# Attention on one core: x transposed by its own DMA, weights loaded in pieces, accumulator banks opened by zero passes, five more tiles on VectorE

## The chip, the cores and the metric

The kernel runs on one core of one Trainium2 chip. The metric is device time in microseconds (us), the median of several executions. "Span" is the time from the first to the last instruction of the one execution that was profiled; it is about 1.8 us shorter than the time that the same execution is given in the list of times. In the lines of the profile PE is TensorE, ACT is ScalarE, DVE is VectorE and SP is SyncE; a q behind the name stands for the engine's sequencer.

## The reference

Sixteen heads of 28 columns each, over 2048 rows of x:

```
x: (1, 2048, 448) bf16, wqkv: (448, 1344) bf16, wo: (448, 448) bf16
qkv = x @ wqkv                     # q, k, v: 16 heads x 2048 x 28
scores = q k^T * 28**-0.5
p = softmax(scores)
out = (p @ v) @ wo
```

## The kernel before

The program is a list of operations with dependencies. A small scheduler in the kernel's own source puts them in order for each engine at build time, so a change in one place can reorder all engines.

The work is cut into 16 units (four heads, 512 query rows), each unit into 16 x 4 tiles of 128 keys x 512 queries. There are 1024 tiles in all. TensorE makes the scores of a tile. ScalarE takes the exponential of two or three tiles with one instruction; VectorE computes it for single tiles by a polynomial of seven operations. TensorE then multiplies the result by V into the unit's accumulator bank (below: the weighted sum).

Before the first exponential can run, x and the weights have to come in, x has to be transposed, and Q and K of the first unit have to be computed. Before the change the transposing is TensorE's work, and the results are copied out of the accumulator memory by VectorE and ScalarE:

```python
XG = 4
xv = xf.rearrange("(n p) d -> p n d", p=128)
...
    dma_x.append(P.add("sp", (lambda e: e.dma_start(x_nat[:, n0:n1, :], xv[:, n0:n1, :])), ...))      # 4 loads of 512 rows
for t, en, prio in ((1, "act", -20), (0, "act", -19), (2, "sp", -7.5)):                               # K, Q, V weights, whole
    dma_w[t] = P.add(en, (lambda e, t=t: e.dma_start(w_raw[0:IT, :, t * D:(t + 1) * D], wview[:, :, t * D:(t + 1) * D])), ...)
...
def tr_job(n0, it, prio, eng):
    def f(e, b):
        for j in range(4):
            ins = e.transpose(bank_bf(b)[0:IT, j * 128:(j + 1) * 128],
                              x_nat[:, n0 + j, it * IT:(it + 1) * IT], id_b[:, :])
        return ins
    xt_ev[(it, n0 // 4)] = job(f"xT{it}_{n0}", prio, [(f, [id_b_op, dma_x[n0 // 4]], "f", 1.1)], ..., evac_eng=eng, ...)
```

TensorE starts slow in these traces: in the kernel before, the first matmuls of zeros start every 0.43 us in groups of four, and every 0.21 us once the clock's own record sets in, at full speed, at 5.25 us. Such a group is here called a zero pass: four matmuls that add nothing to a bank. They are there to get the clock up and to keep it up. Nine passes stand at the start. Others are put into TensorE's idle gaps, and only while some accumulator bank is open: a bank is opened by the operation that has `opens` set and shut by the last sum of its unit.

```python
def zeros(e, b, start, n):
    for i in range(n):
        for h in range(4):
            ins = e.matmul(ps[32 * h:32 * h + 32, b * 512:(b + 1) * 512], ZW[:, :], ZM[:, :], start=start and i == 0, stop=False, ...)
    return ins
warm = P.add("pe", lambda e: zeros(e, 7, True, NWARM), deps=[ms_zw, ms_zm], ..., name="DUMW")      # NWARM = 9
...
def fill(self, zeros, bank_of):
    for k, op in enumerate(pe):
        if k and cur is not None:          # a gap is filled only while a bank is open
            ...
        if op.opens:
            cur = op
        if op.shuts:
            cur = None
...
op = P.add("pe", f_pv, ..., name=f"PV{u}_{kt}", acq=(("M" if u else "A0", 1) if kt == 0 else None), ...)
op.opens = kt == 0                         # the unit's first weighted sum opens its bank
op.shuts = kt == NK - 1
```

At its end the kernel checks its own result (a flag), and every engine branches on it: past the fallback program if the flag is good. A hint, some operations ahead of the branch, announces it:

```python
HINT = {"pe": 40, "act": 8, "dve": 12, "pool": 0, "sp": 4}
...
def body(e, eng):
    n = len(F.order[e])
    F.emit_engine(e, eng, fs, 0, max(n - HINT[e], 0))
    hint = eng.mark_branch_hint_location() if HINT[e] is not None else None
    F.emit_engine(e, eng, fs, max(n - HINT[e], 0), n)
    eng.wait_ge(fs["dve"], F.flag_op.count)
    ok = eng.value_load(F.flag_ap)
    eng.br_ne(ok, 0, f"done_{e}", f"redo_{e}").branch_hint(hint)
    with nc.body(f"redo_{e}", ...):
        ...                                # the fallback program
    nc.switch_bb(f"done_{e}")
```

## Time and profile before

| | us |
|---|---|
| median (424.91 to 425.98, 3 runs) | 425.12 |
| span of the profiled run | 423.67 |
| head: start to the first exponential | 10.87 |
| stream: start of the first exponential to the end of the last | 401.97 |
| tail: from there to the end of the span | 10.83 |

The division into head, stream and tail is read from ScalarE's records. It carries the whole argument, because ScalarE is the limit for the whole stream. First the page of the profiled run: the span, the chain of waits by engine, and the group of ScalarE's exponentials (line, engine, operation, output<-input, shapes, count | busy us, mean ns | idle us before them and what ended it).

```profile
span 423.7 us, 10347 instructions
...
ACT 94%; PE 3%; DVE 1%; issue 0%
...
L842 ACT ACTIVATE PT<-ps 128x1536 bf16<-128x1536 f32 (+1 forms) x309 | 402.0, 1932 | 1.1 <-PE ps L826 1.1
```

ScalarE makes 94% of the chain and is idle 1.1 us in all before its 309 exponentials. The page's mean of one (1932 ns) counts overlap with the next; the starts of two neighbours lie 1.330 us apart for three tiles and 0.903 us for two (medians of the records). The groups kept apart by form show how many there are of each kind:

```profile
L842 ACT ACTIVATE PT<-ps 128x1536 bf16<-128x1536 f32 x278 | 373.7, 2016 | 0.0
...
L842 ACT ACTIVATE PT<-ps 128x1024 bf16<-128x1024 f32 x31 | 28.5, 1179 | 1.1 <-PE ps L826 1.1
```

The two-tile form is the dearer one for each tile: 0.452 us against 0.443 us. Now the start of the chain that ended last (start us, us, what):

```profile
1.21 4.96 PE ps L450 x52
6.17 0.07 issue
6.25 0.42 PE ps L500 x4
6.66 0.02 issue
6.68 0.44 DVE xT L488
...
7.65 1.94 PE ps L517 x32
9.59 0.02 issue
9.61 0.70 DVE KT L488
...
10.45 0.45 PE ps L826 x4
10.89 393.09 ACT PT L842 x303
```

L450 are the zero passes, L500 the transposes of x, L517 the first projections, L826 the first scores. The landings in the trace's DMA records put the first 512 rows of x at 6.11 us. The end is read from what SyncE, which ends the program, waited for (engine, line, what it waited for: us in total, times, longest us):

```profile
SPq L1577 <- PEq L1577: 3.4, 1, 3.4
```

This is the barrier at the end. The view names TensorE's sequencer. The instruction records say otherwise: VectorE came last. Its branch ended at 419.15 us and its next instruction, a drain, started at 423.39 us, 4.24 us later. ScalarE took 0.41 us for the same step.

### The profile page before, as it was taken

The page shows a single profiled execution, that of the slowest core. Times are in us where ns is not written, and L with a number is a line of the kernel's source. Part 1 is how long each engine was busy: PE and PEld are TensorE (multiplying, and loading weights), DVE is VectorE, ACT ScalarE, POOL GpSimd, SP SyncE. Part 2 cuts the span into 40 slices and gives each one's busy share as a digit, 9 for nine tenths or more (in the row PEclk, how much of TensorE's full clock was granted, in tenths as well). Part 3 has the DMA queues.
Part 4 walks back from the last instruction along what each step waited for, and adds up shares of the span by engine and source line. Part 5 has one row for each costly group of instructions (what it writes and reads, how often), then busy time and mean ns, then how long its engine had stood idle before and what let it go on. Part 6 is the DMA issues. An engine that isn't in the chain of part 4 may idle for free.

```text
span 423.7 us, 10347 instructions
## 1 busy us (share of the span) xinstructions
PE 389.0 (92%) x4566; PEld 123.7 (29%) x4566; DVE 380.9 (90%) x650; ACT 406.6 (96%) x316; POOL 3.4 (1%) x9
## 2 busy tenths in 40 slices
PE   8999899999999899899999989998999999999992
PEld 3442232332223233233323222222322223222220
DVE  3436999999999999999999999999999999999953
ACT  2999999999999999999999999999999999999991
POOL 3000000000000000000000000000000000000000
PEclk9999999999999999999999999999999999999997
DMA  8200010101001000010101001010100102010101
GB/s 255 68 0 2 10 26 3 27 2 29 2 4 27 2 27 2 8 22 4 27 3 29 2 3 27 3 28 24 48 3 2 37 15 48 2 29 12 35 27 48
DMA packets 13849, 10.28 MB, mean 24 GB/s; under 512 B 5932, under 2 KB 11820, under 8 KB 13800
## 3 DMA queue, kind: packets, MB, share of 16 engines
q1 hardware_dynamic: 12872, 8.78, 7.7%
q10 hardware_dynamic: 928, 0.80, 0.7%
q8 instruction: 36, 0.59, 0.6%
q14 instruction: 13, 0.11, 0.1%
HBM read 7.50 MB, written 2.08 MB: 23 GB/s over the span
## 4 chain that ended last, share of the span: by engine, by line
ACT 94%; PE 3%; DVE 1%; issue 0%
ACT PT L842 94%; PE ps L450 1%; PE ps L678 1%; PE ps L517 0%; PE ps L773 0%; PE ps L500 0%; PE ps L826 0%; DVE ONX L720 0%; DVE KT L488 0%; DVE OUTS L702 0%; DVE OX L717 0%; DVE xT L488 0%; DVE OTN L722 0%; DVE ZM L444 0%; DVE RS L719 0%
## 5 line engine op out<-in xcount | busy, mean ns | idle before, releaser
L842 ACT ACTIVATE PT<-ps 128x1536 bf16<-128x1536 f32 (+1 forms) x309 | 402.0, 1932 | 1.1 <-PE ps L826 1.1
L826 PE MATMUL ps<-QT,KT 28*128 28x512 bf16 x1024 | 154.6, 384 | 20.5 <-ACT PT L842 15.6
L450 PE MATMUL ps<-ZM,ZW 128*32 128x512 bf16 x1620 | 122.9, 389 | 1.2 <-DVE ZM L444 1.2
L869 DVE TENSOR_SCALAR DT<-ps 128x512 int32<-128x512 f32 x128 | 87.8, 686 | 5.9 <-PE ps L826 4.8
L773 PE MATMUL ps<-PT,V 128*32 128x512 bf16 x896 | 82.2, 384 | 3.0 <-DVE PD L890 1.5
L826 PEld LDWEIGHTS ps<-QT,KT 28*128 28x128 bf16 x1024 | 38.8, 91 | 155.9 <-ACT PT L842 118.9
L890 DVE SCALAR_TENSOR_TENSOR PD<-DT,DL 128x1024 int16<-128x1024 int32 x64 | 77.8, 1216 | 0.0
L450 PEld LDWEIGHTS ps<-ZM,ZW 128*32 128x32 bf16 x1620 | 33.0, 96 | 57.0 <-issue 44.0
L773 PE MATMUL ps<-PD,V 128*32 128x512 bf16 x128 | 46.9, 385 | 0.2
L887 DVE TENSOR_TENSOR DL<-DQ,DL 128x1024 f16<-128x1024 f16 x64 | 43.8, 684 | 0.6
L879 DVE TENSOR_SCALAR DW<-DT 128x1024 f16<-128x1024 uint16 x64 | 43.9, 686 | 0.1
L881 DVE TENSOR_TENSOR DQ<-DW 128x1024 f16<-128x1024 f16 x64 | 43.4, 678 | 0.1
L517 PE MATMUL ps<-xT,w_raw 112*32 112x512 bf16 x512 | 36.8, 383 | 1.0 <-DVE DT L869 1.0
L773 PEld LDWEIGHTS ps<-PT,V 128*32 128x32 bf16 x896 | 20.6, 94 | 38.9 <-issue 17.7
L883 DVE TENSOR_SCALAR DL<-DW 128x1024 f16<-128x1024 f16 x64 | 26.6, 415 | 0.0
L885 DVE TENSOR_SCALAR DQ<-DQ 128x1024 f16<-128x1024 f16 x64 | 26.5, 414 | 0.0
L678 PE MATMUL ps<-wop,OTN 128*128 128x448 bf16 x64 | 15.8, 356 | 2.3 <-DVE OTN L722 1.9
L488 DVE CAST KT<-ps 128x512 bf16<-128x512 f32 x16 | 11.0, 687 | 7.4 <-PE ps L517 7.3
L534 PE MATMUL ps<-w_raw,xT 112*128 112x112 bf16 x256 | 17.1, 214 | 0.0
L488 DVE CAST V<-ps 128x448 bf16<-128x448 f32 x16 | 9.9, 616 | 6.9 <-PE ps L534 6.9
L517 PEld LDWEIGHTS ps<-xT,w_raw 112*32 112x32 bf16 x512 | 10.8, 95 | 16.5 <-issue 7.0
L534 PEld LDWEIGHTS ps<-w_raw,xT 112*128 112x128 bf16 x256 | 13.0, 98 | 6.5 <-issue 4.1
(39 smaller groups left out, 89.3 us busy)
## 6 DMA issues: line engine op xcount, KB each, us to landing
RB<-scr_r SPq DMA_DIRECT2D x60, 64.0 KB, 2.1
x_nat<-in_x_dram SPq DMA_DIRECT2D x4, 448.0 KB, 7.7
out_dram<-OUTS SPq DMA_DIRECT2D x16, 112.0 KB, 1.7
w_raw<-in_wqkv_dram ACTq DMA_DIRECT2D x2, 392.0 KB, 5.6
w_raw<-in_wqkv_dram SPq DMA_DIRECT2D x1, 392.0 KB, 8.8
wop<-in_wo_dram SPq DMA_DIRECT2D x16, 24.5 KB
scr_l<-OTS SPq DMA_DIRECT2D x15, 8.0 KB
LT<-scr_l SPq DMA_DIRECT2D x15, 8.0 KB, 1.7
```

Source lines behind the costliest of these rows:

```text
L450: ins = e.matmul(ps[32 * h:32 * h + 32, b * 512:(b + 1) * 512], ZW[:, :], ZM[:, :], start=start and i == 0, stop=False, tile_position=(0, ...
L517: ins = e.matmul(ps[32 * h:32 * h + 32, b * 512:(b + 1) * 512], w_raw[0:IT, it, col:col + 32], xT[0:IT, it, c * 512:(c + 1) * 512], start= ...
L534: ins = e.matmul(ps[:, b * 512 + j * GD:b * 512 + (j + 1) * GD], xT[0:IT, it, n * 128:(n + 1) * 128], w_raw[0:IT, it, 2 * D + g * GD:2 * D ...
L773: ins = e.matmul(ps[32 * h:32 * h + 32, b * 512:(b + 1) * 512], V[:, kt, hh * 32:(hh + 1) * 32], p_ap, start=(kt == 0 and u > 0), stop=(kt ...
L826: ins = e.matmul(bank(b), KT[32 * h:32 * h + rows, g, kt * 128:(kt + 1) * 128], QT[32 * h:32 * h + rows, g, c * QCH:(c + 1) * QCH], start= ...
L842: ex = P.add("act", (lambda e, p0=p0, w=w, b0=b0: e.activation(PT[:, p0 * 512:(p0 + w) * 512], bank(b0, w), AF.Exp, scale=ESCALE)), deps=[ ...
L869: o1 = P.add("dve", (lambda e, T=T, s=s: e.tensor_scalar(T, bank(s.banks[0]), ZLO, -ZLO, ALU.max, ALU.add)), deps=[s, d_last[di]], dur=610 ...
L879: o2 = P.add("dve", (lambda e, F16=F16, W=W: e.tensor_scalar(W, F16, 1.0 / 65536.0, -0.5, ALU.mult, ALU.add)), deps=[d[2] for d in d_open] ...
L881: o3 = P.add("dve", (lambda e, W=W, Q=Q: e.tensor_tensor(Q, W, W, ALU.mult)), deps=[o2], dur=70 + 540 * k2, prio=pr, name=f"D3_{gi}")
L883: o4 = P.add("dve", (lambda e, W=W, L=L: e.tensor_scalar(L, W, EB, EA, ALU.mult, ALU.add)), deps=[o2], dur=70 + 270 * k2, prio=pr, name=f" ...
L887: o6 = P.add("dve", (lambda e, Q=Q, L=L: e.tensor_tensor(L, Q, L, ALU.mult)), deps=[o4, o5], dur=70 + 540 * k2, prio=pr, name=f"D6_{gi}")
L890: o7 = P.add("dve", (lambda e, T=T, L=L, out=out: e.scalar_tensor_tensor(out, T, 1.0 / 512.0, L, ALU.mult, ALU.add)), deps=[o6] + [slot_la ...
```

## The change

The intent: spare TensorE the transposes and VectorE and ScalarE the copies, bring the weights of the first unit first, let VectorE take five tiles more (133) and keep the first unit's exponentials wider, keep TensorE's clock up by more zero passes, and announce VectorE's branch earlier. The diff, cut to its core:

```diff
-    FILL_TARGET = 0.45
+    FILL_TARGET = 0.48
+    FILL_EARLY = 0.7
+    FILL_UNTIL = 15000.0
-    NWARM = 9
+    NWARM = 16
-        x_nat = sb("x_nat", [128, NST, D], BF16)
-            dma_x.append(P.add("sp", (lambda e: e.dma_start(x_nat[:, n0:n1, :], xv[:, n0:n1, :])), ...
-        for t, en, prio in ((1, "act", -20), (0, "act", -19), (2, "sp", -7.5)):
-            dma_w[t] = P.add(en, (lambda e, t=t: e.dma_start(w_raw[0:IT, :, t * D:(t + 1) * D], ...
+        for c in range(NCH):
+            P.add("sp", (lambda e, rows=rows: e.dma_start_transpose(xT[:, 0:NIT - 1, rows], xf[rows, 0:128 * (NIT - 1)])), ...
+            dma_x.append(P.add("sp", (lambda e, rows=rows: e.dma_start_transpose(xT[:, NIT - 1, rows], xf[rows, XL:D])), ...
+        ...                                   # Q and K weights of the first four heads: ScalarE's queue, first
+        load_w("v", 2 * D, 3 * D, "act", -28)
+        load_w("k", D + W0, 2 * D, "sp", -15)
+        load_w("q", W0, D, "sp", -14)
-        def tr_job(n0, it, prio, eng): ...    # transposes, copies and the identity are gone
-        dve_load[0] += 22.0
+        dve_load[0] += 8.0
-            return ((2, 2), (3, 2), (3, 3))[phase(cur[0])][k % 2]
+            return ((3, 2), (3, 2), (3, 3))[phase(cur[0])][k % 2]
-                                   p_ap, start=(kt == 0 and u > 0), stop=(kt == NK - 1), ...
+                                   p_ap, start=False, stop=(kt == NK - 1), ...
+            if kt == 0 and u:
+                op0 = P.add("pe", (lambda e: zeros(e, acc(u), True, 1)), deps=early_ev + mid_ev, after=[last_pv[0]], ...
+                            name=f"OPEN{u}", acq=("M", 1), acq_slack=ASLACK)
+                op0.opens = True
-HINT = {"pe": 40, "act": 8, "dve": 12, "pool": 0, "sp": 4}
+HINT = {"pe": 40, "act": 8, "dve": 30, "pool": 0, "sp": 4}
```

Left out are the pools of banks in the first unit, the padded layout of the weights (448 rows as three blocks of 128 and one of 64, with zeros from GpSimd), and a correction of the scheduler's times.

More of the change, by code (lines that the diff above doesn't have):

```diff
@@ L204, in schedule @@
                     lat = self.SYNC_LAT
-                ready_t[u] = max(ready_t[u], done_t + lat + (ops[u].slack if isdep else 0.0))
+                ready_t[u] = max(ready_t[u], (done_t if isdep else op.t1) + lat + (ops[u].slack if isdep else 0.0))
                 npred[u] -= 1
@@ L245, in fill @@
                     lo = min(activity(mid - f * self.FILL_SPAN, mid + (1 - f) * self.FILL_SPAN) for f in (0.15, 0.5, 0.85))
-                    if lo + n * one / self.FILL_SPAN >= self.FILL_TARGET:
+                    if lo + n * one / self.FILL_SPAN >= (self.FILL_EARLY if mid < self.FILL_UNTIL else self.FILL_TARGET):
                         break
@@ L330, in _fast @@
     G = H // 4
-    IT = 112
-    NIT = D // IT
+    NIT = 4
+    XL = D - 128
+    W0 = 120
     NST = S // 128
@@ L347, in _fast @@
     ESCALE = 1.0 / (65536.0 * LOG2E)
-    assert DH * H == D and G * 4 == H and DH + 1 <= 32 and NIT * IT == D and GD <= IT
+    assert DH * H == D and G * 4 == H and DH + 1 <= 32 and 128 * (NIT - 1) + 64 == D and GD + 4 <= W0
     xf = x.rearrange("b s d -> (b s) d")
@@ L384, in _fast @@
         OUTS = sb("OUTS", [128, NOB, D], BF16)
-        iota_i = sb("iota_i", [128, 128], I32)
-        id_f = sb("id_f", [128, 128], FP32)
-        id_b = sb("id_b", [128, 128], BF16)
         CK1 = sb("CK1", [128, NU * 16], FP32)
@@ L404, in i32v @@
             return ap.bitcast(I32)
-        XG = 4
-        xv = xf.rearrange("(n p) d -> p n d", p=128)
-        wview = wqkv.rearrange("(it p) c -> p it c", p=IT)
         dma_x = []
-        def load_x(i, prio):
-            n0, n1 = i * NST // XG, (i + 1) * NST // XG
-            dma_x.append(P.add("sp", (lambda e: e.dma_start(x_nat[:, n0:n1, :], xv[:, n0:n1, :])),
-                               dur=400, prio=prio, name=f"dma_x{i}", dma_group=_DmaGroup(f"x{i}"), nbytes=(n1 - n0) * 128 * D * 2))
@@ L416, in _fast @@
-        for i in range(XG):
-            load_x(i, -10 + i)
-        dma_w = {}
-        for t, en, prio in ((1, "act", -20), (0, "act", -19), (2, "sp", -7.5)):
-            dma_w[t] = P.add(en, (lambda e, t=t: e.dma_start(w_raw[0:IT, :, t * D:(t + 1) * D], wview[:, :, t * D:(t + 1) * D])),
-                             dur=400, prio=prio, name=f"dma_w{t}", dma_group=_DmaGroup(f"w{t}"), nbytes=D * D * 2)
-        io_op = P.add("pool", lambda e: e.iota(iota_i[:, :], [[1, 128]], base=0, channel_multiplier=-1),
-                      dur=300, prio=-12, name="iota")
@@ L426, in _fast @@
-        id_f_op = P.add("dve", lambda e: e.tensor_scalar(id_f[:, :], iota_i[:, :], 0.0, None, ALU.is_equal),
-                        deps=[io_op], dur=250, prio=-10, name="id_f")
-        id_b_op = P.add("dve", lambda e: e.tensor_copy(id_b[:, :], id_f[:, :]), deps=[id_f_op], dur=150, prio=-10, name="id_b")
+        for c in range(NCH):
+            rows = slice(c * QCH, (c + 1) * QCH)
+            grp = _DmaGroup(f"x{c}")
+            P.add("sp", (lambda e, rows=rows: e.dma_start_transpose(xT[:, 0:NIT - 1, rows], xf[rows, 0:128 * (NIT - 1)])),
+                  dur=500, prio=-20 + c, name=f"dma_xa{c}", dma_group=grp, nbytes=QCH * 384 * 2)
+            dma_x.append(P.add("sp", (lambda e, rows=rows: e.dma_start_transpose(xT[:, NIT - 1, rows], xf[rows, XL:D])),
+                               after=[P.ops[-1]], dur=500, prio=-20 + c, name=f"dma_xb{c}", dma_group=grp, nbytes=QCH * 128 * 2))
@@ new lines, in _fast, with load_w @@
+        dma_w = {}
+        def load_w(key, c0, c1, en, prio):
+            grp = _DmaGroup(f"w{key}")
+            wv = wqkv[0:128 * (NIT - 1), c0:c1].rearrange("(it p) c -> p it c", p=128)
+            P.add(en, (lambda e: e.dma_start(w_raw[:, 0:NIT - 1, c0:c1], wv)), dur=400, prio=prio, name=f"dma_wa{key}", dma_group=grp, nbytes=(c1 - c0) * 768)
+            dma_w[key] = P.add(en, (lambda e: e.dma_start(w_raw[64:128, NIT - 1, c0:c1], wqkv[128 * (NIT - 1):D, c0:c1])),
+                               after=[P.ops[-1]], dur=400, prio=prio, name=f"dma_wb{key}", dma_group=grp, nbytes=(c1 - c0) * 128)
@@ new lines, in _fast @@
+        grp0 = _DmaGroup("w0")
+        for t in range(2):
+            wv0 = wqkv[0:128 * (NIT - 1), t * D:t * D + W0].rearrange("(it p) c -> p it c", p=128)
+            w0a = P.add("act", (lambda e, t=t, wv0=wv0: e.dma_start(w_raw[:, 0:NIT - 1, t * D:t * D + W0], wv0)), after=P.ops[-1:] if t else [], dur=400, prio=-30,
+                        name=f"dma_w0a{t}", dma_group=grp0, nbytes=W0 * 768)
+        wv1 = wqkv[128 * (NIT - 1):D, 0:2 * D].rearrange("p (t c) -> p t c", t=2)[:, :, 0:W0]
+        wd1 = w_raw[64:128, NIT - 1, 0:2 * D].rearrange("p (t c) -> p t c", t=2)[:, :, 0:W0]
@@ L429, in _fast @@
+        dma_w["q0"] = dma_w["k0"] = P.add("act", (lambda e: e.dma_start(wd1, wv1)), after=[w0a], dur=400, prio=-30, name="dma_w0b", dma_group=grp0, nbytes=2 * W0 * 128)
+        load_w("v", 2 * D, 3 * D, "act", -28)
+        load_w("k", D + W0, 2 * D, "sp", -15)
+        load_w("q", W0, D, "sp", -14)
+        ms_w = P.add("pool", lambda e: e.memset(i32v(w_raw[0:64, NIT - 1, :]), 0), dur=800, prio=-12, name="ms_w")
         V4 = V.rearrange("p n (hh r) -> p (n hh) r", r=32)
@@ L440, in _fast @@
                 dma_wo.append(P.add("sp", (lambda e, g=g, r0=r0, p0=p0: e.dma_start(wop[p0:p0 + DH, g, :], wo[r0:r0 + DH, :])),
-                                    deps=[ms_wop], after=dma_wo[-1:] + dma_x[-1:], dur=300, prio=-5, name=f"dma_wo{g}{h}", dma_group=grp_wo))
+                                    deps=[ms_wop], after=dma_wo[-1:] + [dma_x[-1], dma_w["q"]], dur=300, prio=-5, name=f"dma_wo{g}{h}", dma_group=grp_wo))
         ms_zw = P.add("dve", lambda e: e.memset(i32v(ZW[:, :]), 0), dur=60, prio=-30, name="ms_zw")
@@ L452, in zeros @@
             return ins
-        warm = P.add("pe", lambda e: zeros(e, 7, True, NWARM), deps=[ms_zw, ms_zm], kind="c", units=2.0 * NWARM, prio=-30, name="DUMW")
+        warm = P.add("pe", lambda e: zeros(e, 7, True, NWARM), deps=[ms_zw, ms_zm], kind="c", units=1.0 * NWARM, prio=-30, name="DUMW")
         warm.opens = True
-        P.pool("E", [4, 5, 6])
-        P.pool("J", [5, 6])
+        warm.cells = 1.0 * NWARM
+        P.pool("E", [5, 6])
         P.pool("M", [6, 7])
@@ L463, in _fast @@
         mid_ev = []
-        cur_pool = ["J"]
+        cur_pool = ["E"]
         gated = []
@@ L492, in job @@
             return ev
-        xt_ev = {}
-        def tr_job(n0, it, prio, eng):
-            def f(e, b):
-                ins = None
-                for j in range(4):
-                    ins = e.transpose(bank_bf(b)[0:IT, j * 128:(j + 1) * 128],
-                                      x_nat[:, n0 + j, it * IT:(it + 1) * IT], id_b[:, :])
-                return ins
-            xt_ev[(it, n0 // 4)] = job(f"xT{it}_{n0}", prio, [(f, [id_b_op, dma_x[n0 // 4]], "f", 1.1)],
-                                       ((lambda: xT[0:IT, it, n0 * 128:(n0 + 4) * 128]), (lambda b: bank_bf(b)[0:IT, 0:512])),
-                                       True, evac_eng=eng, evac_dur=600 if eng == "act" else 420)
         kq_ev = {}
@@ L510, in proj_qk @@
             dst = KT if t == 1 else QT
+            wk = "qk"[t] + ("0" if g == 0 else "")
             mms = []
@@ L516, in f @@
                         col = t * D + g * GD + h * DH
-                        ins = e.matmul(ps[32 * h:32 * h + 32, b * 512:(b + 1) * 512], w_raw[0:IT, it, col:col + 32],
-                                       xT[0:IT, it, c * 512:(c + 1) * 512], start=(it == 0), stop=(it == NIT - 1), tile_position=(0, 32 * h))
+                        ins = e.matmul(ps[32 * h:32 * h + 32, b * 512:(b + 1) * 512], w_raw[:, it, col:col + 32],
+                                       xT[:, it, c * 512:(c + 1) * 512], start=(it == 0), stop=(it == NIT - 1), tile_position=(0, 32 * h))
                     return ins
-                mms.append((f, [xt_ev[(it, c)]] + ([dma_w[t]] if it == 0 else []), "c", 1.0))
+                mms.append((f, ([dma_x[c], ms_w, dma_w[wk]] if it == 0 else []), "c", 1.0))
             kq_ev[(t, g, c)] = job(f"p{t}_{g}_{c}", prio, mms,
@@ L533, in f @@
                     for it in range(NIT):
-                        ins = e.matmul(ps[:, b * 512 + j * GD:b * 512 + (j + 1) * GD], xT[0:IT, it, n * 128:(n + 1) * 128],
-                                       w_raw[0:IT, it, 2 * D + g * GD:2 * D + (g + 1) * GD], start=(it == 0), stop=(it == NIT - 1))
+                        ins = e.matmul(ps[:, b * 512 + j * GD:b * 512 + (j + 1) * GD], xT[:, it, n * 128:(n + 1) * 128],
+                                       w_raw[:, it, 2 * D + g * GD:2 * D + (g + 1) * GD], start=(it == 0), stop=(it == NIT - 1))
                     return ins
-                mms.append((f, [xt_ev[(it, c)] for it in range(NIT)] + [dma_w[2]], "f", 1.1))
+                mms.append((f, [dma_x[c], ms_w, dma_w["v"]], "f", 1.1))
             Vd = V[:, 4 * c:4 * c + 4, g * 128:(g + 1) * 128].rearrange("p n (h r) -> p n h r", r=32)[:, :, :, 0:DH]
@@ L540, in proj_v @@
                                ((lambda: Vd), (lambda b: bank(b)[:, 0:4 * GD].rearrange("p (n h d) -> p n h d", n=4, d=DH)), ms_v1), early, evac_dur=600)
-        for c in range(NCH):
-            for it in range(NIT):
-                tr_job(4 * c, it, -3 + 0.25 * c + 0.001 * it if c == 0 else 0.25 * c - 0.35 + 0.001 * it, "act" if (c == 0 and it % 2) else "dve")
-            if c == 0:
-                proj_qk(0, 0, 0, -2.9, True, "act")
-                proj_qk(1, 0, 0, -2.8, True, "dve")
-            else:
-                proj_qk(1, 0, c, 0.25 * c - 0.3, True)
+        proj_qk(0, 0, 0, -2.9, True, "act")
+        proj_qk(1, 0, 0, -2.8, True, "dve")
+        proj_v(0, 0, -0.1, True)
+        for c in range(1, NCH):
+            proj_qk(1, 0, c, 0.25 * c - 0.3, True)
             proj_v(0, c, 0.25 * c - 0.1, True)
@@ L613, in flush @@
             if cur:
-                b0 = ((0, 2), (0, 3), (0, 3))[phase(cur[0])][k % 2]
+                b0 = ((0, 3), (0, 3), (0, 3))[phase(cur[0])][k % 2]
                 items.append(("A", list(cur), b0))
@@ L773, in f_pv @@
                     ins = e.matmul(ps[32 * h:32 * h + 32, b * 512:(b + 1) * 512], V[:, kt, hh * 32:(hh + 1) * 32],
-                                   p_ap, start=(kt == 0 and u > 0), stop=(kt == NK - 1), tile_position=(0, 32 * h))
+                                   p_ap, start=False, stop=(kt == NK - 1), tile_position=(0, 32 * h))
                 return zeros(e, b, False, nd_) if nd_ and not kt else ins
+            if kt == 0 and u:
+                op0 = P.add("pe", (lambda e: zeros(e, acc(u), True, 1)), deps=early_ev + mid_ev, after=[last_pv[0]], kind="c", units=1.0,
+                            prio=u + 1.5 / NK, name=f"OPEN{u}", acq=("M", 1), acq_slack=ASLACK)
+                op0.u = u
+                op0.opens = True
+                last_pv[0] = pv_first[u] = op0
             op = P.add("pe", f_pv, deps=list({id(tile_ev[(u, kt, h)]): tile_ev[(u, kt, h)] for h in range(4)}.values())
-                       + [v_ev[(g, kt // 4)]] + (early_ev + mid_ev if kt == 0 and u else []),
+                       + [v_ev[(g, kt // 4)]],
                        after=[last_pv[0], warm], kind="c", units=1.0 + nd_, prio=u + (kt + 4) / NK, name=f"PV{u}_{kt}",
-                       acq=(("M" if u else "A0", 1) if kt == 0 else None), acq_slack=ASLACK if u else 0.0)
+                       acq=(("A0", 1) if kt == u == 0 else None))
             last_pv[0] = op
             op.u = u
-            op.opens = kt == 0
+            op.opens = kt == u == 0
             op.shuts = kt == NK - 1
-            if kt == 0:
+            if kt == u == 0:
                 pv_first[u] = op
@@ L814, in _fast @@
                 make_late([t for t in todo_late if t[0] >= LATE1 - 0.25])
-            if ph > 0 or kind == "D":
+            if ph > 0:
                 deps += early_ev
@@ L862, in _fast @@
                 s = P.add("pe", (lambda e, tl=tl, hold=hold: s_mm(e, tl, [hold[0].banks[0]], DH)), deps=deps, after=[partner] + d_gate,
-                          kind="r", units=1.0, heads=(tl[0][2],), prio=p_pr + 0.0001, name=f"SD{gi}", acq=("M" if ph == 2 else "J", 1), acq_slack=ASLACK)
+                          kind="r", units=1.0, heads=(tl[0][2],), prio=p_pr + 0.0001, name=f"SD{gi}", acq=("M" if ph == 2 else "E", 1), acq_slack=ASLACK)
                 hold.append(s)
```

## The prediction

> **What bounds it now.** ScalarE. In the chain of waits, exponentials (PT<-ps) are 94% of the span, from 10.87 us to about 410.2 us, and the groups of instructions show 1.1 us of ScalarE idle before all 309 of them. So: head 10.87 us, stream 399.2 us, tail about 13.5 us. The timeline gives 0.921 us per two-tile exponential (22 in 20.27 us); the 278 three-tile ones then take 1.333 us each. VectorE is 90% busy, but in the windows from 10.9 to 38 us it is idle more than half the time. TensorE's clock is granted at 0.994: more zero passes can buy nothing there.
>
> **Stream.** Running the diff's tile split by hand: VectorE gets 133 tiles (6 in the first unit instead of 2), ScalarE 891. With widths 3,2 in the first unit there are 289 three-tile and 12 two-tile exponentials: 385.2 + 11.1 = 396.3 us, so -2.9 us, all on the critical path. VectorE pays 5 x about 2.5 us, gets back 14 xT copies (5.9 us) and the identity (1.8 us), and has early idle time for the rest. I expect ScalarE to stay gapless.
>
> **Head.** Now: x lands near 6.1 us, transposes and copies to 7.65, eight projection passes to 9.6, K copy 0.7, scores 0.45. The change removes the 1.4 us of transposes, but the first x chunk now comes through the transposing DMA as 524 KB instead of 459 KB in two instructions, and 16 zero passes stand before the projection: in the trace such a pass started every 0.43 us until about 5.3 us and every 0.21 us after, so they end near 6.7 us, later if the gap filler adds some. [...] Estimate: projection starts between 6.7 and 7.8 us, exponentials 3.2 us later, about 10.3: -0.5 us.
>
> **Tail.** The last flag is written at 418.2 us. Every engine then loads it and branches (the trace's records): ScalarE, GpSimd and TensorE drain within 0.5 us of their branch, but VectorE branches at 419.15 and drains only at 423.39, and the end barrier waits for it (SyncE 3.4 us, by the queue's waits). Its branch hint came at 414.04, 5 us ahead; ScalarE's, SyncE's and TensorE's came 14 us and more ahead. [...] Hinting 30 instructions ahead instead of 12 puts it near 398 us. SyncE, done at 420.28, becomes last: -3.0 us, if the hint is what was late (three in four).
>
> **Zero passes that open banks.** 15 x 0.21 us of TensorE, which is not critical; the earlier claim on one of two M banks may delay VectorE tiles slightly. About 0.
>
> **Total.** 425.1 - 2.9 - 0.5 - 3.0 = 418.7, and with the chance that one part fails 419.0 us, range 416.6 to 422.4. Chances: faster by over 2% 0.09, within 2% 0.88, slower 0.03.
>
> **What would show it.** Stream: 301 exponentials of 396 us together, no idle. Head: first exponential at 9.5 to 11 us. Tail: VectorE's drain within 1 us of its branch. It is wrong if transposed x lands after about 9 us (head longer), if ScalarE waits in the first unit because two banks now serve projections and VectorE tiles together, or if VectorE's late drain stays.

## The result and the profile after

Ratios are computed as the mean time of one kernel's fast runs over the mean of the other's fast runs of the same rounds, so they are not quite the ratio of the medians quoted.

The changed kernel takes 423.25 us (median of 4; 422.85 to 423.85) against 425.22 us for the kernel before in the same rounds (424.91 to 425.98): ratio 0.9952, interval 0.9934 to 0.9971. That is half a per cent faster. It is outside the predicted range, on the slow side.

| us, profiled runs | before | after | difference | predicted difference |
|---|---|---|---|---|
| head | 10.87 | 12.12 | +1.25 | -0.5 |
| stream | 401.97 | 399.33 | -2.64 | -2.9 |
| tail | 10.83 | 9.75 | -1.08 | -3.0 |
| span | 423.67 | 421.19 | -2.47 | -6.4 |

One pair of profiles carries some spread in the head (the experiments give it a size). The stream and the tail come from long sums and from one large event. The page after, the same lines as before:

```profile
span 421.2 us, 10430 instructions
...
ACT 94%; PE 3%; DVE 1%; issue 0%
...
L841 ACT ACTIVATE PT<-ps 128x1536 bf16<-128x1536 f32 (+1 forms) x301 | 399.3, 1937 | 1.5 <-PE ps L825 1.5
```

And the groups kept apart by form:

```profile
L841 ACT ACTIVATE PT<-ps 128x1536 bf16<-128x1536 f32 x289 | 390.1, 1971 | 1.5 <-PE ps L825 1.5
...
L841 ACT ACTIVATE PT<-ps 128x1024 bf16<-128x1024 f32 x12 | 13.6, 1137 | 0.0
```

Exactly 289 three-tile and 12 two-tile exponentials, as the prediction had counted. The 1.5 us of idle is the wait before the first one. The spacings are the same as before, 1.330 and 0.903 us, and the sum of all that exceeds them is 3.3 us after and 3.4 us before. The stream did what was expected of it.

The head did not. The start of the chain that ended last, after:

```profile
1.21 7.85 PE ps L458 x90
9.06 1.76 PE ps L513 x31
10.82 0.02 issue
10.85 0.70 DVE KT L496
11.55 0.14 issue
11.68 0.41 PE ps L825 x3
12.10 0.02 issue
12.12 390.91 ACT PT L841 x295
```

The transposes and their copies are gone, but zero passes (L458) fill the time until about 9 us. There are 92 matmuls of them before the first projection, that is 23 passes and not the 16 of the diff: the gap filler added seven. The DMA issues of the first microseconds show what else happened (start us, us, engine, line, operation, output<-input):

```profile
0.73 1.41 SPq L411 DMA_TRANSPOSE xT<-in_x_dram  x1
...
2.20 1.24 SPq L413 DMA_TRANSPOSE xT<-in_x_dram  x1
2.50 0.60 ACTq L420 DMA_DIRECT2D w_raw<-in_wqkv_dram  x1
...
3.48 1.98 SPq L411 DMA_TRANSPOSE xT<-in_x_dram  x1
```

A transposing DMA holds SyncE for 1.24 to 2.11 us in this trace, where a plain load of x took 0.46 to 0.58 us in the one before; all of x had landed at 16.27 us, against 12.70 us. The second one, which completes the first 512 rows, is issued at 2.20 us. Right behind it ScalarE's queue issues the V weights (L420), which nobody needs yet. The first 512 rows of x land at 8.03 us, 1.92 us later than before.

The barrier at the end after:

```profile
SPq L1576 <- PEq L1576: 2.3, 1, 2.3
```

It is 1.1 us shorter. In the records VectorE's gap between branch and drain has shrunk from 4.24 to 0.52 us, as predicted. But ScalarE's has grown from 0.41 to 3.45 us: its branch ended at 417.41 us and its drain came at 420.87 us. ScalarE now closes the program.

### The profile page after: what moved, and what is told of

It reads as the page before. It is cut to its first block, busy times and chain, and to the rows that moved or that the text cites. A ratio compares the mean times of both kernels' runs of the same rounds, so it can differ in the third digit from the quotient of the medians.

```text
span 421.2 us, 10430 instructions
## 1 busy us (share of the span) xinstructions
PE 389.1 (92%) x4602; PEld 122.4 (29%) x4602; DVE 385.5 (92%) x657; ACT 402.7 (96%) x306; POOL 3.7 (1%) x9
## 4 chain that ended last, share of the span: by engine, by line
ACT 94%; PE 3%; DVE 1%; issue 0%
ACT PT L841 94%; PE ps L458 2%; PE ps L671 1%; PE ps L513 0%; PE ps L825 0%; DVE OX L710 0%; DVE ONX L713 0%; DVE KT L496 0%; DVE OUTS L695 0%; PE ps L766 0%; DVE OTN L715 0%; DVE ZM L452 0%; DVE RS L712 0%; PE ps L928 0%; DVE FLAG L932 0%
## 5 line engine op out<-in xcount | busy, mean ns | idle before, releaser
L458 PE MATMUL ps<-ZM,ZW 128*32 128x512 bf16 x1720 | 130.1, 390 | 1.9 <-DVE ZM L452 1.2
L889 DVE SCALAR_TENSOR_TENSOR PD<-DT,DL 128x1024 int16<-128x1024 int32 (+1 forms) x67 | 81.1, 1210 | 0.0
L458 PEld LDWEIGHTS ps<-ZM,ZW 128*32 128x32 bf16 x1720 | 36.5, 97 | 61.6 <-issue 42.0
L886 DVE TENSOR_TENSOR DL<-DQ,DL 128x1024 f16<-128x1024 f16 (+1 forms) x67 | 45.7, 682 | 0.7
L878 DVE TENSOR_SCALAR DW<-DT 128x1024 f16<-128x1024 uint16 (+1 forms) x67 | 45.8, 683 | 0.0
L880 DVE TENSOR_TENSOR DQ<-DW 128x1024 f16<-128x1024 f16 (+1 forms) x67 | 45.2, 675 | 0.1
L513 PE MATMUL ps<-xT,w_raw 128*32 128x512 bf16 x512 | 35.6, 382 | 0.2 <-DVE DT L868 0.2
L884 DVE TENSOR_SCALAR DQ<-DQ 128x1024 f16<-128x1024 f16 (+1 forms) x67 | 27.9, 417 | 0.0
L882 DVE TENSOR_SCALAR DL<-DW 128x1024 f16<-128x1024 f16 (+1 forms) x67 | 27.8, 415 | 0.0
L530 PE MATMUL ps<-w_raw,xT 128*128 128x112 bf16 x256 | 17.8, 214 | 0.1
L530 PEld LDWEIGHTS ps<-w_raw,xT 128*128 128x128 bf16 x256 | 13.1, 98 | 8.6 <-issue 5.0
L513 PEld LDWEIGHTS ps<-xT,w_raw 128*32 128x32 bf16 x512 | 10.8, 95 | 16.0 <-issue 7.0
```

Source lines behind the costliest of these rows:

```text
L530: ins = e.matmul(ps[:, b * 512 + j * GD:b * 512 + (j + 1) * GD], xT[:, it, n * 128:(n + 1) * 128], w_raw[:, it, 2 * D + g * GD:2 * D + (g ...
L878: o2 = P.add("dve", (lambda e, F16=F16, W=W: e.tensor_scalar(W, F16, 1.0 / 65536.0, -0.5, ALU.mult, ALU.add)), deps=[d[2] for d in d_open] ...
L880: o3 = P.add("dve", (lambda e, W=W, Q=Q: e.tensor_tensor(Q, W, W, ALU.mult)), deps=[o2], dur=70 + 540 * k2, prio=pr, name=f"D3_{gi}")
L884: o5 = P.add("dve", (lambda e, Q=Q: e.tensor_scalar(Q, Q, -0.25, None, ALU.add)), deps=[o3], dur=70 + 270 * k2, prio=pr, name=f"D5_{gi}")
L886: o6 = P.add("dve", (lambda e, Q=Q, L=L: e.tensor_tensor(L, Q, L, ALU.mult)), deps=[o4, o5], dur=70 + 540 * k2, prio=pr, name=f"D6_{gi}")
L889: o7 = P.add("dve", (lambda e, T=T, L=L, out=out: e.scalar_tensor_tensor(out, T, 1.0 / 512.0, L, ALU.mult, ALU.add)), deps=[o6] + [slot_la ...
```

## The experiments

Three questions: what decides whether an engine stalls after the branch, what holds the head, and what the x transposing DMA and the zero passes are worth in the stream. All twelve kernels gave correct results. Besides the times they are compared by head, stream and tail of their profiled run.

### The tail: the hint's lead, or the branch's place

Two theories. Lead (the prediction's): the hint must come early enough, and ScalarE's, eight operations ahead, has become too late. Place: what counts is where the branch stands in the engine's own instruction stream. In the built program I count an engine's instructions up to the branch (waits counted, a matmul as two); this count is called the place below. The change moved VectorE's place from 698 to 711 (it has more tiles, and fewer copies), and ScalarE's from 327 to 320 (it has fewer exponentials and copies). Nobody intended either. The recorded expectations give the place less a round number, 640 on VectorE and 256 on ScalarE: 58 stands for 698, 71 for 711 or 327, 64 for 320 and 72 for 328.

**ScalarE's hint 24 operations ahead, on the kernel after.**

```diff
-HINT = {"pe": 40, "act": 8, "dve": 30, "pool": 0, "sp": 4}
+HINT = {"pe": 40, "act": 24, "dve": 30, "pool": 0, "sp": 4}
```

> After, with ScalarE's branch hint 24 instead of 8 operations before its end, nothing else. In the changed kernel ScalarE drains 3.45 us after its branch and is last at the end barrier. LEAD theory (the one of the prediction: a hint must come early enough): ScalarE then drains about 0.4 us after its branch, SyncE's drain at about 418.9 us is last, span 421.2 -> about 419.2 us, 0.5% less than the changed kernel. PLACE theory (what counts is where in the engine's instruction stream[...] the branch falls: 56 to 64 stalled, 69 to 72 did not, in the four cases at hand): the branch does not move, so the gap stays at 3.5 us and the span at about 421.2.

Measured: 422.3 us, ratio to before 0.9925 (0.9902 to 0.9949). The hint was given at 381.55 us, 36 us ahead of the branch, and ScalarE still stalled 2.49 us. So the lead isn't what is short. The stall was 1 us shorter than in the kernel after; why is open.

**Eight tiny ScalarE instructions at the start, hint unchanged, on the kernel after.** They move the place from 320 to 328 and cost nothing, as ScalarE waits for x then.

```diff
+        PADS = sb("PADS", [128, 1], BF16)
+        pad = None
+        for i_ in range(8):
+            pad = P.add("act", lambda e: e.activation(PADS[:, :], ZW[:, 0:1], AF.Identity), deps=[ms_zw, pad], ...)
```

> After, with 8 one-column ScalarE activations added in ScalarE's idle time before its first real work (5 to 10 us), so that every later ScalarE instruction stands 8 places further on; the hint stays 8 operations before the end, its lead in time the same 14.4 us. LEAD: gap after ScalarE's branch stays 3.5 us, span about 421.2. PLACE: the branch moves from place 64 to 72[...], the gap falls to about 0.4 us and the span to about 419.2.

Measured: 420.62 us, ratio 0.9876 (0.9856 to 0.9895). ScalarE's gap is 0.42 us, the tail 7.66 us. The barrier's wait in this run:

```profile
SPq L1580 <- PEq L1580: 0.2, 1, 0.2
```

The tail is two microseconds shorter for eight instructions that do nothing, as the place theory expected for ScalarE.

**The change's own hint, alone, on the kernel before.**

```diff
-HINT = {"pe": 40, "act": 8, "dve": 12, "pool": 0, "sp": 4}
+HINT = {"pe": 40, "act": 8, "dve": 30, "pool": 0, "sp": 4}
```

> Before, with VectorE's hint 30 instead of 12 operations before its end, the part of the change that the prediction gave 3.0 us to. LEAD: VectorE drains within 0.6 us of its branch instead of 4.2, span 423.7 -> about 420.7, ratio about 0.993. PLACE: VectorE's branch stays at place 58[...], the gap stays about 4.2 us, the span at about 423.7, ratio 1.000.

Measured: 425.36 us, ratio 1.001 (0.9972 to 1.0047). VectorE's hint moved from 414.04 to 397.33 us and the gap went from 4.24 to 3.94 us. The barrier's wait hardly changed:

```profile
SPq L1577 <- PEq L1577: 3.0, 1, 3.0
```

This is the step of the prediction done by itself. The lead theory had expected a ratio of 0.993, which lies outside the interval; no gain shows.

**The change's hint undone, on the kernel after.**

```diff
-HINT = {"pe": 40, "act": 8, "dve": 30, "pool": 0, "sp": 4}
+HINT = {"pe": 40, "act": 8, "dve": 12, "pool": 0, "sp": 4}
```

> After, with VectorE's hint back at 12 operations before its end (about 5 us of lead, as in before). LEAD: VectorE stalls about 4 us again and drains near 421.9, the span goes from 421.2 to about 422.3. PLACE: VectorE's branch stands at place 71, no stall, gap about 0.5 us, span about 421.2 (ScalarE last, as in after).

Measured: 422.95 us, ratio 0.9947 (0.9916 to 0.9977), the same as the kernel after. The hint came 5 us ahead of the branch again, and VectorE's gap stayed at 0.52 us.

**Thirteen tiny VectorE memsets at the start of the kernel before**, which move its place from 698 to 711; hint unchanged.

```diff
+        PADD = sb("PADD", [128, 2], BF16)
+        pad_v = None
+        for i_ in range(13):
+            pad_v = P.add("dve", lambda e: e.memset(i32v(PADD[:, :]), 0), deps=[pad_v], ...)
```

> Before, with 13 tiny VectorE memsets added in its idle first microseconds: VectorE's branch moves from place 58[...] to place 71; the hint stays 12 operations and about 5 us ahead. PLACE: the gap after VectorE's branch falls from 4.2 to about 0.5 us, SyncE's drain near 420.3 is last, span 423.7 -> 420.7, ratio about 0.993. LEAD (already shaken by the four runs before): gap and span unchanged.

Measured: 423.0 us, ratio 0.9925 (0.9876 to 0.9975). The gap is 0.52 us and the tail 7.83 us, 3.0 us shorter than before:

```profile
SPq L1581 <- PEq L1581: 0.2, 1, 0.2
```

That is the whole gain that the prediction had put on the hint. The head of this profile was 11.62 us, longer than before's 10.87, because TensorE's clock rose only after the last zero pass; so the span shows 2.25 us of the 3.

The readings of the step from branch to drain in these runs (in the later ones VectorE stands at place 711 or 721 and ScalarE at 327 or 328, and no gap is over 0.52 us):

| engine | kernel | place | hint ahead of the branch | gap, us |
|---|---|---|---|---|
| VectorE | before | 698 | 5.1 us | 4.24 |
| VectorE | before, hint 30 | 698 | over 20 us | 3.94 |
| VectorE | after | 711 | over 20 us | 0.52 |
| VectorE | after, hint 12 | 711 | 5 us | 0.52 |
| VectorE | before, 13 memsets | 711 | 5 us | 0.52 |
| ScalarE | before | 327 | 15 us | 0.41 |
| ScalarE | after | 320 | 14 us | 3.45 |
| ScalarE | after, hint 24 | 320 | 36 us | 2.49 |
| ScalarE | after, hint 12 for VectorE | 320 | 14 us | 3.15 |
| ScalarE | after, 8 tiny instructions | 328 | 14 us | 0.42 |

TensorE shows something like it in another form: there the branch itself takes longer. It took 0.39 to 0.49 us with 9146 or 9218 instructions ahead (in the last three runs 9219 and 9354), and 2.30 and 2.02 us in the two runs with 9170 (the next two runs below); filled up to 9218 again, it took 0.39 us. So in these runs the count of instructions ahead of a branch decides, and they show which counts were bad on which engine; they give no rule for other counts.

Why a place is bad was not shown. The traces give one more sign. The queues that the page calls "instruction" move packets of 16,384 and 8,192 bytes (36 and 0.59 MB on the one, 13 and 0.11 MB on the other in the kernel before). Between the hints and the branches, the kernel after has one packet of the smaller kind (404.1 us), and the run with the eight tiny instructions has two (404.0 and 404.35 us). The same holds in all 14 traces: between 370 us and the branches the five with a stalled VectorE or ScalarE have one packet of the smaller kind, the nine others two. So the second packet and the missing stall go together. But the records don't say which engine a packet of that queue belongs to, and no packet of that kind ends within the last 0.4 us before a late drain. What ends the stall isn't seen, and the mechanism stays open.

### The head: too many zero passes, or x landing late

Two theories for the 1.25 us. Zero passes: 23 passes before the first projection keep TensorE until about 8.9 us. Landing: x lands at 8.03 us instead of 6.11, because the V weights on ScalarE's queue move beside it (from 2.50 to 8.03 us the trace has packets of both queues, both booked on the core's 16 DMA engines, at a DMA share of 1.17); fewer passes then gain little.

**Nineteen passes instead of 23**, with the eight tiny ScalarE instructions.

```diff
-    FILL_EARLY = 0.7
+    FILL_EARLY = 0.48
-    NWARM = 16
+    NWARM = 13
```

> After with the 8 ScalarE pads of t2_actpad (its control: first exponential 11.81 us, 23 zero passes ahead of the first projection, x landed 8.53), and 19 zero passes instead of 23. ZERO-PASS theory (the head grew because zero passes hold TensorE until 8.7 us): projections start near 7.6 to 8.0 us, first exponential 10.8 to 11.2. X-LANDING theory (the head grew because the transposed x lands at 8.0 to 8.5 instead of 6.0 us): projections start at the landing, first exponential 11.2 to 11.8, gain over t2_actpad at most 0.5 us.

Measured: 423.24 us, ratio 0.9945 (0.9894 to 0.9997). The first exponential started at 11.53 us; x landed at 8.25 and the first projection started at 8.29 us. The total was spoiled by the tail: the 24 matmuls fewer (48 in this count) put TensorE's branch at 9170, and the branch took 2.30 us. In this run, and in the next, one of SyncE's last two stores of the output also took 2.17 and 1.45 us to issue, against 0.45 us; that stays unexplained.

**The V weights held back until x has landed**, on top of that.

```diff
+        [o for o in P.ops if o.name == "dma_wav"][0].deps.append(dma_x[0])
```

> h1_fewer, with ScalarE's queue holding back the 401 KB of V weights until x's first 512 rows have landed. SHARE theory (the second transposing DMA of the first chunk is late because the V weights share the DMA engines with it): it lands near 7 us, projections start at 7.3 to 8.0, first exponential 10.5 to 11.2. OWN theory (issue of 1.4 us each and the small packets of the transposing DMA itself): it still lands at 7.8 us or later, first exponential 11.2 us or later.

Measured: 422.46 us, ratio 0.9925 (0.9872 to 0.9977). x landed at 6.38 us and the projections started at 6.70 us, 1.6 us earlier than in the run above. So the V weights beside it were what made x late. But the first exponential came only at 11.49 us: ScalarE, which issues those loads, was itself stuck in the wait for x, and its copy of Q came late. A bad way to do the right thing.

**Nineteen passes, with TensorE's branch put back** by 24 tiny matmuls.

```diff
+                if kt == 8 and u in (3, 4, 5, 6, 7, 8):
+                    for h in range(4):
+                        ins = e.matmul(ps[32 * h:32 * h + 32, b * 512:b * 512 + 8], ZW[:, :], ZM[:, 0:8], start=False, stop=False, ...)
```

> h1_fewer (whose TensorE branch took 2.3 us instead of 0.5 and whose tail was 9.7 us, though ScalarE and VectorE no longer stalled), with 24 eight-column zero matmuls spread over six later score-value products, so that TensorE's branch stands at the same place in its instruction stream as in t2_actpad. PLACE for TensorE too: its branch takes about 0.5 us again, the tail is 7.7 us, and with a first exponential near 11.5 us the span is about 418.7, ratio to before about 0.987. If the longer tail of h1_fewer has another cause, it stays near 9.7 and the span near 420.6.

Measured: 420.87 us, ratio 0.9876 (0.9848 to 0.9905), just the ratio of the run with 23 passes and the eight tiny instructions. TensorE's branch took 0.39 us. The passes ended at about 6.7 us and TensorE then waited: x landed at 8.65 us, the first projection started at 8.70 us. Four passes fewer gain nothing while x is late.

**The V weights issued behind ScalarE's own early work, after x.**

```diff
+        hold_v = [o for o in oa if o.name in ("dma_wav", "dma_wbv")]
+        hold_v[0].deps.append(dma_x[0])
+        ...                                   # moved behind the eight tiny instructions in ScalarE's order
```

> h2_vlate mended: V weights held back until x's first 512 rows have landed, but with ScalarE's table load and pads before that wait, so that its copy of Q is not held up (in h2_vlate x landed at 6.4 us, projections started at 6.7, yet ScalarE was busy with these), and with TensorE's branch put back as in h1p_place. SHARE theory: x lands near 6.4 us again (8.0 to 8.5 in five runs with the V weights let through), projections start by 7 to 8 us (zero passes end then), first exponential at 10.0 to 11.2 us, span 417.2 to 418.5, ratio to before 0.983 to 0.986. If the early landing in h2_vlate was chance: 8 us or later, first exponential 11.2 or later.

Measured: 421.43 us, ratio 0.9895 (0.9861 to 0.993). x landed at 6.17 us, but in this profile TensorE's clock rose late, at 6.91 us, so that the passes ran until 8.1 us and the first exponential came at 11.35 us. With x early, the passes do bind. The times of this kernel spread widely (419.73 to 423.29 us).

**Only the V weights of the first four heads early**, the rest later on SyncE's queue; nineteen passes; every branch at its good place.

```diff
-        load_w("v", 2 * D, 3 * D, "act", -28)
+        load_w("v0", 2 * D, 2 * D + GD, "act", -28)
+        load_w("v", 2 * D + GD, 3 * D, "sp", -14.5)
```

> After with the pads, 19 zero passes, and the V weights of the first head group alone (100 KB) loaded early, the other 300 KB after x. SHARE theory: x's first rows land at 6.4 to 7.2 us and the first exponential is at 10.2 to 11.4 us; the values' projections need no late weights, so ScalarE does not wait in the first unit. Places of all branches as in t2_actpad, tail 7.7 us, span 417 to 418.7, ratio 0.982 to 0.987. OWN theory (the transposing DMA's own issue time): landing 7.8 or later, first exponential 11.2 or later.

Measured: 418.87 us (418.74 to 419.10, 6 runs), ratio 0.9831 (0.9805 to 0.9858). x landed at 6.60 us, the projections started at 6.70 us. The first exponential and the barrier of this run:

```profile
9.92 3.71 ACT L854 ACTIVATE PT<-ps 128x1536 bf16<-128x1536 f32 x3 [1.54 <-PE ps L838]
```

```profile
SPq L1589 <- PEq L1589: 0.2, 1, 0.2
```

Head 9.92, stream 399.33, tail 7.68 us. This version beats both kernels, and it is the steadiest of all. Against the run with 19 passes and the place mended, whose clock rose at the same 4.0 us, x landed 2.05 us earlier and the first exponential came 2.02 us earlier: that much of the head was the landing.

| profiled run | passes before the projections | x's first rows landed | first projection | first exponential |
|---|---|---|---|---|
| before | 13 | 6.11 (not transposed) | 7.65 | 10.87 |
| after | 23 | 8.03 | 8.89 | 12.12 |
| 19 passes, place mended | 19 | 8.65 | 8.70 | 11.94 |
| V weights behind x | 19 | 6.17 | 8.12 | 11.35 |
| V weights in two parts | 19 | 6.60 | 6.70 | 9.92 |

How much of the 1.25 us is spread of the runs? The three profiles with before's head (before itself, the longer hint, the memsets) have the first exponential at 10.65 to 11.62 us, the four with the change's (after and the runs with the hints and with the eight tiny instructions) at 11.61 to 12.12 us. So the change lengthened the head by about 0.8 us (mean of each group; the groups just touch). The spread goes with the instant at which TensorE's clock rises: the clock's own records put it between 3.89 and 7.09 us in the 14 traces (5.25 us before, 6.73 us after), though the passes start at 1.21 us in every one, and the latest one came after the zero passes.

### What the transposing DMA gives the stream

**x loaded and transposed as before, the rest of the change kept.** VectorE keeps its early tiles but has to copy the transposed x again. The weights too are loaded whole, as before, and ScalarE has its eight tiny instructions; so the run with 23 passes and these instructions is the control.

```diff
-            P.add("sp", (lambda e, rows=rows: e.dma_start_transpose(xT[:, 0:NIT - 1, rows], xf[rows, 0:128 * (NIT - 1)])), ...
-            dma_x.append(P.add("sp", (lambda e, rows=rows: e.dma_start_transpose(xT[:, NIT - 1, rows], xf[rows, XL:D])), ...
+            dma_x.append(P.add("sp", (lambda e: e.dma_start(x_nat[:, n0:n1, :], xv[:, n0:n1, :])), ...
+        ...                                   # transposes, copies, whole weights, NWARM 9 as before
```

> After with the 8 ScalarE pads, but x loaded as in before and transposed by TensorE, with before's weight loads: the change without its DMA transpose. If the transposing DMA is what lengthened the head, the first exponential is back near 10.8 us; with the stream of about 399.4 us and the tail of 7.7 us of t2_actpad the span is about 417.9, 1.1 us less than t2_actpad, ratio to before about 0.986. If the head was lengthened by the other parts (banks, zero passes, three-tile first exponential), it stays near 11.8 and the span near 419. VectorE's 14 more copies might also make ScalarE wait in the first unit: then the stream is above 400 us.

Measured: 423.31 us, ratio 0.9945 (0.9895 to 0.9995). Head 11.36, stream 402.18, tail 7.96 us. The head and the tail stand near the control's 11.81 and 7.66 us, but the stream lost all of its gain in one wait of ScalarE in the first unit (its waits from 26 to 34 us):

```profile
ACT PT L855 <- PE ps L839: 2.8, 1, 2.8
```

There the scores waited for transposes, and the transposes for copies that stood behind VectorE's tiles. So in the stream the transposing DMA pays by making room on VectorE for the early tiles; this rests on one profile. In the head it does not pay as the change was written (11.81 us in the control, 11.36 here). With the V weights out of its way it does: 9.92 us.

### What the opening passes are worth

**The best version without the fifteen passes that open the banks**; the first sum of each unit opens its bank, as before. Tiny instructions keep all branches at their places.

```diff
-            if kt == 0 and u:
-                op0 = P.add("pe", (lambda e: zeros(e, acc(u), True, 1)), ..., name=f"OPEN{u}", acq=("M", 1), acq_slack=ASLACK)
-                ...
-                                   p_ap, start=False, stop=(kt == NK - 1), ...
+                                   p_ap, start=(kt == 0 and u > 0), stop=(kt == NK - 1), ...
-            op.opens = kt == u == 0
+            op.opens = kt == 0
```

> h4_v0 without the fifteen zero passes that open each unit's accumulator bank: the first weighted sum of a unit opens its bank itself, as before the change, and the bank is again claimed by that sum. Three more tiny VectorE memsets and 128 tiny TensorE matmuls in place of 16 keep every engine's branch at the place it has in h4_v0, so that the end of the kernel can't hide or fake an effect. Theory NO-EFFECT (the prediction's): the passes are off the critical path. First exponential within 0.6 us of 9.92 (it moves with TensorE's clock), first to last exponential 399.1 to 399.6 us, tail 7.6 to 7.8 us, ratio to before 0.980 to 0.986 (h4_v0: 0.9831). Theory OPENING (the change's intent): opening the bank early spares ScalarE stalls at the starts of the fifteen units; without it at least 0.1 us per unit comes back, stream 400.8 us or more, ratio 0.986 or more, and the waits of ScalarE show TensorE's scores before its exponentials at the units' borders.

Measured: 424.83 us (422.57 to 425.4, 6 runs), ratio 0.9961 (0.993 to 0.9992). Head 10.86, stream 403.73, tail 8.20 us. The stream is 4.40 us longer than with the passes (399.33). The prediction had expected nothing, and the no-effect theory fell. The head's 0.94 us more goes with the clock, which rose at 5.92 us here and at 4.03 us in the best version, and says nothing of the passes. The two kernels ran in different rounds on different chips, but before's medians there agree (425.82 and 425.81 us). The stretches before and behind the border of the first and the second unit show how, first without the passes (stretch, its length, then busy us and instructions of each engine, the granted clock, the DMA engines' share and GB/s):

```profile
36.00:40.00 4.00, 2.70 (x36) 0.74 (x33) 4.00 (x7) 4.00 (x4) 0.00 (x0) 1.00 0.01 2
40.00:50.00 10.00, 10.00 (x69) 2.06 (x67) 6.87 (x12) 7.76 (x6) 0.00 (x0) 0.50 0.07 18
```

The same two stretches with the passes:

```profile
36.00:40.00 4.00, 3.65 (x50) 1.06 (x46) 4.00 (x8) 4.00 (x5) 0.00 (x0) 1.00 0.02 4
40.00:50.00 10.00, 9.14 (x116) 2.65 (x112) 9.68 (x17) 10.00 (x9) 0.00 (x0) 1.00 0.16 30
```

Without them TensorE was busy 2.70 of 4 us, and then its clock was granted at 0.50 for ten microseconds. ScalarE was busy only 7.76 of those ten. TensorE's own timeline shows the hole:

```profile
38.22 0.39 PE L775 MATMUL ps<-PT,V 128*32 128x512 bf16 x4
38.57 0.39 PE L832 MATMUL ps<-QT,KT 28*128 28x512 bf16 x3
39.91 0.51 PE L832 MATMUL ps<-QT,KT 28*128 28x512 bf16 x3 [0.95 <-ACT PT L848]
40.35 0.62 PE L775 MATMUL ps<-PT,V 128*32 128x512 bf16 x4
```

The last sum of the first unit has shut its bank (38.22 us), the first sum of the second opens the next at 40.35 us, and in between no zero pass can be placed, because no bank is open. The longest single idle of TensorE there was 0.95 us. How much idle is too much stays open: with the V weights held back by ScalarE's wait (the second run of the head's experiments), the clock stayed full through 3.41 us (from 7.45 us) with TensorE busy 0.52 of the time. The drop happened a second time near the end: TensorE was busy 1.59 of the 4 us from 390 us, and then the clock was at 0.50 from 395.0 to 398.5 us. Counted as what the spacings of exponentials exceed their medians, ScalarE lost 3.3 us between 38 and 52 us and 2.4 us in its last 21 us, and 0.0 and 0.05 us there in the version with the passes. The other borders show no such drop. ScalarE's waits for scores in the whole run, first without the passes, then with them (where only the wait before the first exponential is left):

```profile
ACT PT L848 <- PE ps L832: 4.2, 6, 1.5
...
ACT PT L854 <- PE ps L838: 1.5, 1, 1.5
```

The opening theory had the direction, and its lower bound held (stream 400.8 us or more, ratio 0.986 or more), but not its form: it expected a small loss at each of fifteen borders. The trace shows two drops of the clock. All six timed runs had mean clocks of 0.975 to 0.984; all six runs with the passes had 0.996. Taking the passes out also makes the scheduler order the rest anew, so the 4.40 us is what they are worth in this kernel, not in another. Nor do the passes settle the clock by themselves: single runs of other kernels that have them go down to 0.985 (424.74 us, VectorE's hint undone), and the kernel before with thirteen memsets, which has none, stood at 0.994 to 0.998.

The kernel before hints at the same. Of its 36 fast runs beside the experiments, five had a mean clock of 0.981 or 0.982 and took 427.75 to 428.73 us; the other 31 had 0.988 or more and took 424.62 to 426.63 us. No trace of one of the five was taken, so where they lost their time is open.

## Why the prediction was wrong

The bound was right: ScalarE in the stream, and only what shortens head, stream or tail counts. The span fell 3.9 us short of the prediction: 1.9 us in the tail, 1.75 us in the head and 0.3 us in the stream.

- **Stream, predicted -2.9, measured -2.64 us: right.** The count of exponentials was exact, ScalarE stayed gapless, VectorE did the five tiles. The difference is about that of the spacing of two-tile exponentials: predicted from 0.921 us each, where the median is 0.903, which makes 0.34 us for the 19 that went.
- **Tail, predicted -3.0, measured -1.08 us: the step that failed.** "SyncE, done at 420.28, becomes last: -3.0 us, if the hint is what was late". The hint was not what was late. Alone, on the kernel before, it changed nothing (ratio 1.001), and undone on the kernel after it changed nothing either. What counted was how many instructions stand ahead of the branch in each engine's stream (why, stays open). The change moved VectorE's branch to a good count by luck and, unnoticed, ScalarE's to a bad one: 3.72 us gained on one engine, 3.04 us lost on the other. The visible sign (VectorE's drain within 1 us of its branch) came true for another reason, so it could not tell the theories apart.
- **Head, predicted -0.5, measured +1.25 us in the pair, about +0.8 over more profiles: wrong in sign.** The estimate let the first rows of x arrive as early as before and counted 16 passes. They arrive at 8.03 us. Transposing is not the cause: the rows land at 6.2 to 7.0 us in the four traces in which the V weights are held back or cut to a quarter, and at 6.11 us without transposing in the kernel before, though other loads were in flight beside them there. What the prediction left out is what runs beside them: here the V weights on the other queue cost x some 2 us (8.65 us with them, 6.60 us with a quarter of them). The seven passes of the gap filler are the second part: in the profile after they held the projection from 8.03, where x had landed, to 8.89 us. The words "later if the gap filler adds some" were written down and not costed.
- **Opening passes, predicted about 0: not refuted against the kernel before, wrong in reason.** The stream came out as the count of exponentials alone had it, but without the passes the changed schedule loses 4.40 us. "TensorE's clock is granted at 0.994: more zero passes can buy nothing there" took the clock for given. In the changed schedule it fell when these passes were taken out.

With both faults mended, the change gives 418.87 us: head -0.95, stream -2.64, tail -3.15 against before. The sum of the prediction was within reach once the change was mended; the kernel as written did not reach it.

## What to carry to other kernels

When a stall follows a branch, as here (up to 4.24 us), compare the instruction counts of every engine before and after, and try a few empty instructions before believing in a hint; a change that adds or removes instructions can move such a stall from one engine to another (here 3.72 us gained on VectorE, 3.04 us lost on ScalarE). When a load becomes critical, look at every other DMA that is in flight beside it, also those of other queues, and bring only the bytes that the first work needs (here 2.02 us of the head). A clock that stands at full speed in the profile of a tuned kernel may stand there because of work that looks idle, so test such work by taking it out (here the clock fell to 0.50 twice, and the stream was 4.40 us longer).
